# A planned order for four chained attention layers, searched anew: same operations, other orders, engines and banks

## The chip, the cores and the metric

The kernel runs on one core of a Trainium2 chip. The core has five instruction streams that run side by side and meet only through semaphores: TensorE (PE; matrix products into eight PSUM banks), ScalarE (ACT), VectorE (DVE), GpSimd (POOL) and SyncE (SP, which issues most transfers). The metric is device time in microseconds (us) of one execution; lower is better. Times are given as the median of several runs on the same chip.

## What is computed

Four layers with a residual around each, on x of 2048 tokens by 512 features, 32 heads of 16 features:

```python
x = x + A(layernorm(x), A_wqkv, A_wo)
x = x + B(layernorm(x), B_wqkv, B_wo)
x = x + A(layernorm(x), A_wqkv, A_wo)
x = x + B(layernorm(x), B_wqkv, B_wo)
# A, linear attention: phi(t) = where(t > 0, t + 1, exp(t)) + 1e-6
#   kv = sum over tokens of phi(k) v;  z = sum of phi(k);  o = phi(q) kv / (phi(q) z + 1e-6);  o @ wo
# B, sliding window of 256 keys, causal: o = softmax(q k / 4 inside the window) v;  o @ wo
```

## The kernel before, in words

**Tiles.** The 2048 tokens are 16 tiles of 128. A norm (`norm`, L363) is statistics on VectorE (L367, L368), an addition of epsilon on GpSimd or VectorE (L369), a power -1/2 on GpSimd (L370), the scaling on VectorE (L371) and a transposition, which is a DMA transpose that SyncE issues (L377) or, for ten of them, four PE products (L383) with an eviction (L390). Products of a token tile with weights are written by `tok` (L406: two instructions of 512 columns for each half of the contraction) or `feat` (L420: eight of 128 columns for each half). In A layers, keys and queries go through `phi` (exponential on ScalarE L429, then VectorE L430 and L431). In B layers, scores are products in 32-row tiles of PE (L638; the far part of the window L677 or L680), exponentials on ScalarE (L648, L690), masks on VectorE (L656, L700, L709) or GpSimd (L708), values `pv` (L729, up to 24 instructions of 34 columns), a reciprocal and a scaling (L740, L741), the product with wo (L406) and the residual (L574). Keys and values pass through two rearranging transfers each (`kd` L600, `vd` L619). The second B layer streams its finished tiles to the output (L847, L782).

**What sets the order.** Plan builds a graph of 2542 operations, the same in every version: names, what each reads and writes, which engines may do it. `place` (the function printed at the end of this section) then takes from a packed string, TABLE, three things: the global order of the operations, the engine of each, and the PSUM bank of each tile. Each engine runs its own operations in that order; `synchronise` puts a semaphore wait wherever an operation needs another engine's result or the bank that an earlier tile held. SyncE's queue is in order too: a transfer whose wait is not met holds back all behind it. One more wait comes from `place`: a GpSimd operation that is not in the list SHORT waits for the last VectorE operation of the kinds E1, xn, mk, mf that stands ahead of it in the global order.

```python
    order = [ops[raw[2 * k] + 256 * raw[2 * k + 1]] for k in range(n)]
    for o in ops:
        o.eng = ("PE", "ACT", "DVE", "POOL", "SP")[raw[2 * n + o.i]]
    for k, x in enumerate(tiles):
        x.banks = [raw[3 * n + k]]
    for o in order:
        if o.eng == "POOL" and o.name not in SHORT and wide and wide not in o.deps:
            o.deps.append(wide)
        if o.eng == "DVE" and o.name in WIDE:
            wide = o
```

**Names used below.** An operation is called by its name and its number in the order of building: fill0 to fill9 are ten products with no use for the result (L268), which keep PE busy at the start, behind nine more of the same kind (L984); k24 is the first half of the first layer's key product of tile 12 (two instructions, L406), k26 and k27 those of tile 13; T12 is the DMA transpose of tile 12 (L377) and xn12 its scaling (L371); g is the product of normed x and phi(k) (L481); wp0 to wp7 copy and permute B's weights (L355) and zero0 to zero4 clear buffers (L803, L818, L820); s38 and s111 are groups of scores (L638); k40, k41 are key products of the second A layer, bv18, bv19 value products of the first B layer (all L406); spread3 is the product that spreads reciprocals to heads (L556), pqd12 to pqd15 the four VectorE multiplications that read it (L563), bve9 the eviction of bv18 and bv19 (L395); bk52 is a half of a key product of the second B layer (L420, eight instructions); outp0 to outp14 are the output transfers of its first 15 tiles (L847).

Of the kernel before, what the change touches and what calls it, by code (L numbers as in the profile page):

```python
# [223 lines left out]
class Plan:  # L224
# [639 lines left out]
    r"-N}%?_Ew~MLpedY&Gw>S1syz@+B~;(TS-1;7z#BLZ;Z=H72~d$@RTG*)26YbZ!F?D3BViO&1yK*+Eo4-gR3epF{Rlrn1Qk(5QUz5ZRaj+KSyU3G)k84K",
    r"s>rH{DypKWf=~#mKvb1fy@O;bxpFGH8VzHhw#urqsbVU-%Aty@5~`$%rgEyvkW!^kxl}1tTIE({RaI3@l~Gkx0jQ($KwhY;>Zt~*vZ}6XsFtdgYOQLjT",
    r"B^QU18ZR&6ow*D6xyhUs;z3I8mo4yiE6K!tBTN6HB&9rde{Ip-~#M}{cr#}sDm(CjZq=s5j=*uYM!bFW7Rk{QjJm<VVxSU)~iEM5+<mLYQDMzlhgur85",
    r"XJ|s-xPVp1@O>tlq;1n4)H=nQE3=q&BL>YKfYvrm5+wlez+%)Mm9`9aRU^QuPcvt1fDeI;OU$t?Hm!sk*9<uu9c})vBB7u0FvswOj?m;J8A~R=3n~6#|",
    r"2);OdSl1t-)=bxQS6Au$wQRoB#QbzN;!C9ouZhSMs9I;;+<N9wUEh1*p~6-t%H&=>}HsGaJGx~ZaL42+4-)C<*9mBF&OOYK(A)jf4zmBTZtmkNt})LB&",
    r";o~m=|fm)+3sEg{nTB~AX0!)Mn@uez{XYirAq-tU<ysK`gI2aG(Vr@K&=WrCB#|wB7M`IEkgYj{nN`|RaYV}UNS0B_H^-;Z5KdPTpQcR8^AsnVr;V}Y^",
    r"#c?<uBVt;W0uy5etcaDcGVWE8FeRo_bulug!i*RN>){oZ2`{S&I1w9Q6|9Q&F*9bt)OZPF;bp9Y)$o&QhAnV5&cV6Z96zf`_(gqHKP$jS*ch{7Hq4GW@",  # L870
    r"Gf4#?^Hv)hxf4wHpN#;AtK>xH5q?UQ*bJ_!mHQ@b7E_}hS#y2`d;-`jOA5Zte`5YN-7Q3z+9LXJ7X8@iVH9uw#0>)8@pk5%z$|?FXlr*jZrZ_7QjUq4H",
    r"u(9i%YNv&PRvKuqRH#7-}h|$CxUX>V*YyIZnqJ7+b|rE3go*!mYRsx8n|6iG5UGRUOyhIxLL+)Bx2RS7U!w1jEr<T#rSu7>1_^R2(BxB#KP)@EJbG7kC",
    r"4A;x62cd+-N*gEz4<RiU?d3m@SVe29;+5B9~ExEG^PRLY~OQa_AFc~yTLfcaE@)ebx0U7CdhaS%Sm0_q;M$4)pHhv1JGpAt|)x=#buAoU%-#u?NRXJR#",
    r"~PBo||?Zf@}3OC?Jyn_dDCVj%sIEyyn_qYXXQ40EkUvW0gp`Q^bB`HEmMX4zX#iH1hjN;Hx9ENGAHXX#Il$?g+2poy&XfAEW=oEuuQhjPb4=@8A!ozq3",
    r"(^5{#MYpjbJ)lhVkXlkkBFas9s1+rmN0gqJgftz+%(Rl)QXLwsT2mWpPl@RmKBgzMidIuQ>Oeo?dwhrSs4mr`yp)gf(+4a-9jOU5rB2kD3X-9&)Sa5qa",
    r"Xf(^@g#Pm=G2eYQGc38mK+76`LuxI(kVQR184&Ur$RK4TF`nbOkHRb^`IgYf{Icx8bpI>Ej^_nw3&v|7Ro|dX)6_{5>%2F(jr<+*=PxEqwTbmcF;1~NF",
    r"gZ{4N)W1P?eoRQy3~mKhPT*uHMoxwTpIB4%$PBI58*Tq@0Y`P-!YdWhpF`qsCO8l5+~~NiV4vrQ~NcjC#{|G@M4zNE$_r=oRgw*R-Gd&~y5p4$~2OL8I",
    r"v?9is#EiN4Sp9z$bkFYTnYypEgmJNiuTX&il}7Tl5#Q7S%8<LLyQq!08n0r&M@8mH(qt>?^~g@2-~oSJ{6kJO4=a~md3!)aNVIRuB~P@IF?a!wA-nhz3",
    r"kE<QtN=^UM>c07S5QXUS&VR;fwrYV$;^Ko7d$KkmM=jIEvfs1i|UQX$`D6gOl{3HLw@3=h|;6i+nE>UsL#+RuqZ{$rJfy;4cF3%OXAQ$G%+?Ts>f9}9t",
    r"xg!tcPW+xfa7C`fmH7%);eI@T2lF5v!iF7ZXUh>e5@+OK9GRnVRlZ8s=sNY_o*b2X@fIG*qj)Ms<7w1~qw{E<PJ4MD-=O^*gM0HwF2SF;6lda?e3Pnib",  # L880
    r"*{lRxg_u4ojjC>@h%R|lejcb=2~2v4{>*%!ee+Uf9B!5mACN--p;q^HXY_V+>MX$F+Ra{`3u+Mqdbj|b1aU{cPI`|=aYPnm0aK%tR*hbWRzK4hU0ld-~",
    r"gZJQ+$SvSUJtt`37I);1WXWa{~@34f!UY<=cFV@9<qd$WB5_SZT!fcs7TTIoz1%@;v^^;pIL@lwk5RXOrwQmO&!Od|to{c^v1EP_l@da8n-7&G-R7<VX",
    r"CNpKxS}BCVvgw2`B7iKEIfxy*YwJ}2Ob99?$vaY@LFc>*utrTj!#u5b*ACXwW+h=h|ka*gB4Q+~$FcsZ}&n37+f^9z0^&!wPT<=7HW;!6TaD7oZ?6p%!",
    r"cSdvI?$tx!$kDQcKa!$@mEGaBSWF@cS3sOifN^vPFB_*F+lFL#-DoST5A*=bNd?%HpvUHVV(q6hqDXAh=rJLlGYEoU=Nm5BB9i)czmX6X%l1p2uK(FMr",
    r"RHXirLQ+a9NiBV(uk@4er4n_Q9x^}%${_iH-*6g9D{r}{%$51lOXkS}dCA}LD}K%2b7?6ngJp=6k(x47W=Sn6FGFRRq?7bATjoePSt`q9xtx|Wa#m_f9",
    r"a$)grLNSI`qDt&$$R-A86>l;kd?AZ7ReGBE+b^5jFQo^R@TW6vR<;t8`&UN<f^QejFMHZiPCFiqr8<dGFCpyCut~+q_K>X@zO*#$#vN*TjYk^lv{FJ>g",
    r"xu2t8DXLX{5Ky4%sQqrG?y)rqWFA$^_XZtfz_SA7#4yB)eszOp-lvNHWP}nIU^+pG=W^GFA4=0ck1s<*+=EgYr<0$Rl|y_4H@?B3boU$)~gETsptbqx0",
    r"$l`ezBQL+Bhjx6Y|S7u4BwcCEG1g>*yRNEg<fbr)Sk57kyX-B>r#O?5L}R7cdqbXOflht-jEbKOF>)ZO$PJy#FcA$2R=PPf+`bVnUZch{|TC*4Mm(9?B",
    r"j9a;C#J#{bLTesDH^hg~{kJ91v3>`(!)1&nmT};o^vvhIYSC7>Lba*{bm(b(%AU#A6)=_mo-Csx0CG~h+T9?uj^h8}oZ_-<ISv_B0(O30m9mXus3-wmL",
    r"O@}qx^(1{w&(@3db-h@JGdJ{2eM>LV`}AZzMNiX3Oi@$J?AHhM4!ujS)wlId9p0?d>-8NSO&2#MOmrPXf2U*W*E*JdrDN+jI<Agjmg;3XqS>wY>VtZ@j",  # L890
    r";G`6je4qns-Njd=DFUWBbzAZrCy;|>OJ~<{YL+wALxgAmA<P#>d*R-KCBbyg!+j7q!a0qrj&W1SL=KFkiM_K=(r}Hd8>ca$Mp#v-yGGa^%;FqpVB|+$2",
# [179 lines left out]
```

## Time and profile before

| what | value |
|---|---|
| median of 3 runs | 410.21 us (409.73 to 410.4) |
| span of the profiled execution | 408.2 us |
| PE, DVE, ACT, POOL busy in it | 396.0, 347.9, 344.4, 113.8 us |
| PE work (instructions) | 7997 products and as many weight loads |
| transfers | 67654 packets, 37.88 MB |
| instruction packets on queue q8 | 63, of 1.03 MB in all |

The profiled execution has only its span as a time: from the first to the last instruction of the program. The median of the runs is 2.0 us above it; that is what lies around the span. A row of the timeline gives the start, the length, the engine and line, what is written and read, how many instructions were merged, and in brackets the idle time of the engine before it with what ended that. Products on PE overlap: a row of PE begins some 0.17 us before the one ahead of it has ended, so a pause shows as a late start even where the bracket is small.

### The profile page before, as it was taken

How to read it: one execution, taken by the hardware profiler on the slowest of the kernel's cores; microseconds unless marked ns; L12 is line 12 of the kernel's file. 1: busy time of each engine (PE TensorE's matmuls, PEld its weight loads, DVE VectorE, ACT ScalarE, POOL GpSimd, SP SyncE). 2: the span in 40 equal slices, each digit the busy share in tenths (PEclk: the TensorE clock that was granted, in tenths of full speed). 3: DMA queues.
4: the chain of work that ended last, by engine and by line, in shares of the span. 5: the costliest groups of instructions: out<-in, count | busy, mean ns of one | idle time of the engine just before them, and what ended most of it. 6: DMA issues, size and time to landing. Idle time of an engine off the chain costs nothing.

```text
span 408.2 us, 18082 instructions
## 1 busy us (share of the span) xinstructions
PE 396.0 (97%) x7997; PEld 263.4 (65%) x7997; DVE 347.9 (85%) x808; ACT 344.4 (84%) x443; POOL 113.8 (28%) x194
## 2 busy tenths in 40 slices
PE   8999999999999999999999999999999999999996
PEld 3654676666575566666666777676757766576664
DVE  5998799999998999888977789988898778876685
ACT  3655579999999999999998355999998999999992
POOL 3553632112253343330503202122123201302212
PEclk9999999999999999999999999999999999999999
DMA  8754014923242934344231100364225542442543
GB/s 247 243 118 104 2 42 121 184 56 97 65 119 52 132 73 108 75 104 106 62 69 36 29 2 28 89 127 78 71 76 130 143 83 61 66 121 62 118 109 104
DMA packets 67654, 37.88 MB, mean 93 GB/s; under 512 B 48248, under 2 KB 62712, under 8 KB 67576
## 3 DMA queue, kind: packets, MB, share of 16 engines
q1 hardware_dynamic: 67184, 35.67, 38.1%
q8 instruction: 63, 1.03, 1.1%
q0 software_dynamic: 384, 1.05, 0.8%
q14 instruction: 15, 0.12, 0.1%
q10 hardware_dynamic: 8, 0.00, 0.0%
HBM read 6.29 MB, written 2.10 MB: 21 GB/s over the span
## 4 chain that ended last, share of the span: by engine, by line
PE 81%; ACT 10%; DVE 7%; DMA 1%; issue 1%; DVEq 0%
PE ps L406 27%; PE ps L420 20%; PE ps L729 15%; PE ps L638 8%; ACT pb L648 7%; PE ps L680 2%; PE ps L481 2%; ACT pb L690 1%; DVE XQ L563 1%; PE ps L677 1%; DMA XQ<-vp 1%; PE ps L984 1%; PE ps L457 1%; PE ps L543 1%; PE ps L268 1%
## 5 line engine op out<-in xcount | busy, mean ns | idle before, releaser
L648 ACT ACTIVATE pb<-ps 128x1024 bf16<-128x1024 f32 (+3 forms) x224 | 198.2, 966 | 7.4 <-PE ps L638 6.2
L729 PEld LDWEIGHTS ps<-vB,pb 128*128 128x128 bf16 x2560 | 77.6, 96 | 11.5 <-issue 4.2
L729 PE MATMUL ps<-vB,pb 128*128 128x34 bf16 x2560 | 83.2, 177 | 0.3
L420 PE MATMUL ps<-xT,wBp 128*128 128x128 bf16 x1024 | 68.6, 219 | 0.1
L420 PEld LDWEIGHTS ps<-xT,wBp 128*128 128x128 bf16 x1024 | 58.4, 98 | 9.6 <-issue 4.0
L708 POOL TENSOR_SCALAR_AFFINE_SELECT pb<-pb 128x1024 bf16<-128x1024 bf16 x34 | 39.1, 1149 | 84.0 <-DVE pb L700 31.9
L429 ACT ACTIVATE tE<-ps 128x512 bf16<-128x512 f32 x64 | 38.1, 606 | 18.4 <-PE ps L406 12.1
L638 PE MATMUL ps<-XQ,kB 32*128 32x256 bf16 (+2 forms) x1024 | 48.7, 262 | 3.3 <-ACT pb L648 0.6
L574 DVE TENSOR_TENSOR xres<-ps,xres 128x512 bf16<-128x512 f32 x63 | 43.1, 685 | 9.6 <-PE ps L406 9.1
L690 ACT ACTIVATE pb<-ps 128x1024 bf16<-128x1024 f32 x50 | 49.0, 1048 | 1.3 <-PE ps L680 1.0
L406 PE MATMUL ps<-wA,XQ 128*128 128x512 bf16 x192 | 49.2, 380 | 0.7 <-DMA XQ<-vp 0.6
L369 POOL TENSOR_SCALAR ve<-mv 128x1 f32<-128x1 f32 x49 | 11.8, 240 | 127.9 <-DVE mv L368 126.9
L370 POOL TENSOR_TENSOR rs<-ve,negh 128x1 f32<-128x1 f32 x64 | 37.9, 592 | 32.0 <-DVE ve L369 27.5
L367 DVE BATCH_NORM_STATS2 stats<-xres 128x6 f32<-128x512 bf16 x64 | 43.8, 685 | 2.8 <-DMA xres<-in_A_x_dram 2.1
L638 PEld LDWEIGHTS ps<-XQ,kB 32*128 32x128 bf16 x1024 | 15.7, 92 | 31.4 <-ACT pb L648 8.3
L420 PE MATMUL ps<-XQ,wA 128*128 128x128 bf16 x512 | 34.4, 219 | 0.0
L406 PE MATMUL ps<-wBv,xT 128*128 128x512 bf16 x128 | 34.3, 380 | 0.0
L406 PE MATMUL ps<-M,XQ 128*128 128x512 bf16 x128 | 33.3, 380 | 0.2
L420 PEld LDWEIGHTS ps<-XQ,wA 128*128 128x128 bf16 x512 | 30.1, 98 | 5.1 <-issue 0.6
L406 PE MATMUL ps<-wBo,oT 128*128 128x512 bf16 x124 | 32.7, 380 | 0.6 <-DVE vp L431 0.4
L656 DVE TENSOR_TENSOR pb<-pb,tri 128x512 bf16<-128x512 bf16 x68 | 27.7, 419 | 3.7 <-ACT pb L648 3.1
L741 DVE TENSOR_TENSOR o<-ps,rc 128x256 bf16<-128x256 f32 x64 | 27.0, 422 | 1.7
(114 smaller groups left out, 545.9 us busy)
## 6 DMA issues: line engine op xcount, KB each, us to landing
vB<-vS SPq DMA_DIRECT2D x64, 136.0 KB, 2.6
kB<-vp SPq DMA_DIRECT2D x64, 128.0 KB, 2.2
wA<-in_A_wqkv_dram SPq DMA_DIRECT2D x3, 512.0 KB, 5.2
xres<-in_A_x_dram SPq DMA_DIRECT2D x2, 512.0 KB, 4.8
pb<-in_B_wqkv_dram SPq DMA_DIRECT2D x1, 1024.0 KB, 6.9
out_dram<-xres POOLq DMA_DIRECT2D x8, 128.0 KB, 2.5
out_dram<-xres SPq DMA_DIRECT2D x7, 128.0 KB, 2.0
xres<-in_A_x_dram SPq DMA_DIRECT2D x3, 256.0 KB, 5.3
```

Of the source, the lines that this page charges most:

```text
L367: self.on("DVE", "stats", lambda e: e.bn_stats(K.stats[:, t, :], K.xres[:, t, :]), key, dve(512), rd=[("xres", t)], wr=[("stats", t)])
L370: self.pow = self.on("POOL", "pow", lambda e: e.tensor_tensor(K.rs[:, t, :], K.ve[:, t, :], K.negh[:], ALU.pow), key + 0.03, (640, 690), r ...
L406: m = e.matmul(K.ps(ps), lhs(c), rhs(c), start=c == 0, stop=c == 3)
L420: m = e.matmul(K.ps(ps)[:, f * P:(f + 1) * P], w(c, f), xT(c), start=c == 0, stop=c == 3)
L429: self.on("ACT", "E", lambda e: e.activation(K.tE[:, s, :], K.ps(ps), ACT.Exp, bias=0.0), key, act(512), wr=[("tE", s)], ps=[ps])
L574: self.on("DVE", "res", lambda e: e.tensor_tensor(K.xres[:, t, :], K.ps(po), K.xres[:, t, :], ALU.add), key, dve(512), rd=[("xres", t)], w ...
L638: m = e.matmul(K.ps(ps[gq])[:, ns * i:ns * i + ns], K.kB[rows, j % 4, 2 * f + b, :, :], K.XQ[rows, f, q:q + ns], start=True, stop=True, ti ...
L648: return e.activation(out(h, ns).rearrange("p (f g) c -> p f g c", f=n), i, ACT.Exp, bias=0.0, scale=0.25)
L656: return e.tensor_tensor(x, x, K.tri[:, 0, :].unsqueeze(1).to_broadcast([P, 4 * n, 64]), ALU.mult)
L690: return e.activation(o.rearrange("p (f g) b c -> p f g b c", g=2), i, ACT.Exp, bias=0.0, scale=0.25)
L708: return e.affine_select(out=x, in_=x, compare_op=ALU.is_ge, fill=0.0, base=-2, pattern=[[0, 16], [-2, 64]], channel_multiplier=1)
L729: m = e.matmul(K.ps(ps)[:, 34 * u:34 * u + 34], K.P((b // 2) % rp)[:, f, gq % 2 * 2 + gq // 2, o:o + P], K.vB[:, (b // 2) % 4, b % 2, r, : ...
```

## The change

Only TABLE is another string (two lines shorter, so the lines behind it move up by two: L984 is L982). The graph, the emitted instructions' shapes and the waits' rules are the same.

```diff
 TABLE = (
-    r"c-qZa1K1|VvaT*P*0yciwr$(CZQHhO+qTW@CcDXcb7%hV<eVfoo0F4!@AKUGhSk+o?^{*fGyMUCh3765goc+c9E6835CI|rLPAiG2oggihztY|-3#}`C",
...
+    r"c-qx@1GFW{(r!jXMn-1awr$(CZQHhO+qP}nwrykjuj(`X{+YScbMMT%YrXaARPL<(W#9``?y7a3I;BvBQlS;7V2adTci)9jPaG?)j1m=Bg;DpMQxDuj7hHu^",
...
 )
```

Unpacked, and set beside the old one by names:

- **Engines.** 52 operations change engine. By counts (before to after): wp on ACT 6 to 2, on POOL 2 to 6; zero on ACT 3 to 1, on POOL 2 to 4; recb on ACT 5 to 3, on DVE 3 to 5; outp on POOL 8 to 9, on SP 7 to 6; mf on DVE 17 to 16, on POOL 39 to 40; eps on POOL 49 to 48, on DVE 15 to 16; bqe on DVE 22 to 21. In all ACT has 442 to 437 operations, DVE 807 and 807, POOL 190 to 196, SP 235 to 234.
- **PE order.** 868 operations; 88% stand in the same sequence, with the same 333 changes between tile shapes. The ten fills were spread over the first 15 us (two ahead of the first transposition, three between the first two, five behind); now seven stand ahead of the first transposition, two between the first and the second, one behind.
- Sequences on PE at places that are spoken of below (before, then after):

```text
B  g16 q8 q9 g18 k26 g20 k24 k25 k27 g19
A  g16 g18 k26 k27 q8 q9 g20 k24 k25 g19

B  s37 bk21 k40 k41 spread3 bv18 bv19 s38 aout24
A  s37 bk21 bv18 bv19 spread3 k40 k41 s38 aout24

B  pv89 s118 bv50 bv51 s111 bk52 bk53 bq54
A  pv89 s118 bk52 bv50 bv51 s111 bk53 bq54
```

- **VectorE around the second place:** bke10 mk28 pqd15 pqd12 becomes bke10 pqd12 pqd15. s38 waited for both pqd12 and pqd15; now it waits for pqd12, and for bve9 on ScalarE, which stands ahead of E36 instead of behind it.
- **From 345 us on** PE's sequence differs in one place (pv103 ahead of pv100) and ScalarE's in two swaps of neighbours and the operation of the last point below; VectorE's sequence changes in most stretches (286 of its 807 operations lie elsewhere).
- **SyncE, first layer:** the load of A_wo stood behind T7, the third DMA transpose, and now stands behind T12, the ninth; the transposes keep their sequence (T13 ahead of T12).
- **The end.** Before: SP issued outp14 (the last whole tile) and the two halves of tile 15; POOL ended with outp12, outp7, outp13. After: SP issues the two halves alone; POOL ends with outp12, outp13, outp14, outp7. The first eviction of the last transposition (oTe1, L395) moves from ACT to DVE, behind the residual of tile 13 (L574), which moves behind the scaling of the half tile before.

More of the change, by code (lines that the diff above doesn't have):

```diff
@@ L864 @@
[L864 to L879, printed above, removed]
```

90 lines of the change are left out of this document (52 added, 38 removed).

## The prediction

> **What bounds the kernel now.** I read the page first, for the engines' shares, then who waited for whom on PE, then the sums by stretch, and then the timeline at the places that the change touches.
>
> ```profile
> span 408.2 us, 18082 instructions
> PE 396.0 (97%) x7997; PEld 263.4 (65%) x7997; DVE 347.9 (85%) x808; ACT 344.4 (84%) x443; POOL 113.8 (28%) x194
> ```
> ```profile
> 0.00:10.00 10.00, 8.75 (x38) 3.81 (x39) 5.86 (x16) 3.00 (x4) 3.41 (x14) 1.00 0.80 244
> ...
> 400.00:410.00 10.00, 4.72 (x111) 3.34 (x109) 3.93 (x9) 1.46 (x4) 2.38 (x5) 0.99 0.35 107
> ```
>
> The first fence is the page, the second the sums by stretches of 10 us (length; busy time of PE, weight loads, DVE, ACT, POOL; granted clock; share and GB/s of the transfers). PE is busy 396.0 of 408.2 us, so no new order can take away more than the 12.2 us of its idle time. Of these, 10.0 - 8.75 = 1.25 lie at the start and 8.2 - 4.72 = 3.5 at the end, behind the last products, where the order hardly changes. That leaves 12.2 - 1.25 - 3.5 = 7.45 us: the floor is about 410.21 - 7.45 = 402.8.
>
> ```profile
> 115.00:140.00 25.00, 24.10 (x539) 16.16 (x535) 22.14 (x55) 24.90 (x29) 7.45 (x14) 1.00 0.49 90
> 341.50:386.00 44.50, 41.93 (x1175) 29.62 (x1171) 32.69 (x75) 44.02 (x52) 8.99 (x11) 1.00 0.45 97
> ```
>
> These two rows (same columns, other stretches) say that part of the 7.45 is out of reach. From 115 to 140 us ScalarE is busy 24.90 of 25.00, and from 341.5 to 386 us 44.02 of 44.50, while PE idles 0.90 and 2.57: there PE waits because ScalarE is full. The change leaves ScalarE's operations and nearly their sequence there as they are, so what PE gains inside such a stretch it waits for at its next exponential. About 7.45 - 0.90 - 2.57 = 4.0 us are open to a better order.
>
> ```profile
> PE ps L406 <- DMA XQ<-vp: 0.6, 1, 0.6
> ...
> PE ps L638 <- DVE XQ L563: 0.4, 1, 0.4
> ```
>
> Who waited for whom on PE (total, times, longest): no wait above 0.6 us but the start's, and one that names a transfer. So the change is judged wait by wait.
>
> **The change part by part.**
>
> *Transfers and instruction packets.* The landing times do show what the new search is about:
>
> ```profile
> q1 hardware_dynamic: 1697, 0.41, 45.0%
> ...
> XQ<-vp SPq DMA_TRANSPOSE x4, 2.4
> ```
> ```profile
> q8 instruction: 1, 0.02, 2.8%
> ...
> XQ<-vp SPq DMA_TRANSPOSE x2, 3.3
> ```
> ```profile
> DMA to landing us min/median/max: 2.4/2.6/5.3
> ```
>
> The first is the transfers' view from 25 to 29.5 us: four transposes, no packet of queue q8 (q1, their own, is the only queue listed), 2.4 us to landing. The second is from 30.5 to 33.5 us: one q8 packet, and the median of two transposes is 3.3. The third is the source view of all 84 transposes. A transfer that meets a packet is late by about 0.9 us, at most 2.9. PE pays for it at one place:
>
> ```profile
> 29.82 0.41 DVE L371 TENSOR_SCALAR vp<-xres,mv,rs 128x512 bf16<-128x512 bf16 x1
> ```
> ```profile
> 33.66 0.59 PE L481 MATMUL ps<-vp 128*128 128x512 bf16 x2
> 34.84 1.47 PE L406 MATMUL ps<-wA,XQ 128*128 128x512 bf16 x6 [0.59 <-DMA XQ<-vp]
> ```
>
> xn12 ends at 30.23 on VectorE and T12 follows it. Two products take 0.43 (the pair below, 9.28 to 9.71), so k24 could have started at 33.66 + 0.43 = 34.09; it started at 34.84, and 0.75 us went. In the new order k27, one more pair, stands ahead of k24: 0.43 more cover. The A_wo load behind T12 instead of ahead of T8 frees SyncE earlier, but VectorE is the one that T12 waits for: between its gate (the second tile pair's load) and xn12 the new order puts the same work on it. If T12 meets its packet again, 0.75 - 0.43 = 0.32 stay; if not, nothing stays. Bounds of this part: -0.75 to 0; I take **-0.43**.
>
> *The fills.* With two fills ahead, the first transposition started at 5.92. Now seven stand there:
>
> ```profile
> 5.07 1.06 PE L268 MATMUL ps<-kB 128*128 128x512 bf16 x2
> 5.92 0.63 PE L383 MATMUL ps<-ident,vp 128*128 128x128 bf16 x4
> 6.34 1.15 PE L268 MATMUL ps<-kB 128*128 128x512 bf16 x3
> 7.33 0.39 PE L383 MATMUL ps<-ident,vp 128*128 128x128 bf16 x4
> 7.55 1.89 PE L406 MATMUL ps<-wA,XQ 128*128 128x512 bf16 x8
> 9.28 0.59 PE L268 MATMUL ps<-kB 128*128 128x512 bf16 x2
> 9.71 1.06 PE L420 MATMUL ps<-XQ,wA 128*128 128x128 bf16 x16
> 10.61 0.39 PE L383 MATMUL ps<-ident,vp 128*128 128x128 bf16 x4
> ```
>
> The first two take 5.92 - 5.07 = 0.85, the next three 7.33 - 6.34 = 0.99, later ones 0.215. Seven take 0.85 + 0.99 + 0.43 = 2.27, so T0 comes at 7.34, T1 at 7.34 + 0.22 + 0.43 = 7.99, and k0 at 7.99 + 0.22 + 0.215 = 8.42. Before, k0 came at 7.55 with five fills still to pay, 5 x 0.215 = 1.08, which is 8.63 on the same count. PE has no pause up to 34 us in either case, so the moved fills cost and save **0**; bounds -0.2 (8.42 against 8.63) to +0.3 (an exponential later in front of VectorE, which is full there). The Trainium skill, TensorE: Matmul & The Clock Gate, section on the clock gate, says that the warm-up is a budget of about 3.4 us of time and not a number of products; by it fills moved to the front warm nothing sooner. The trace agrees: the pitch goes from 0.43 to 0.215 between 6.3 and 7.3 us, whatever is run. The sum stays 0 by both.
>
> *The scores s38.*
>
> ```profile
> 138.73 1.04 PE L406 MATMUL ps<-wA,XQ 128*128 128x512 bf16 x4
> 139.74 0.40 PE L556 MATMUL ps<-rec,spread 32*128 32x128 bf16 x16
> 140.07 1.04 PE L406 MATMUL ps<-wBv,xT 128*128 128x512 bf16 x4
> 141.54 0.40 PE L638 MATMUL ps<-XQ,kB 32*128 32x256 bf16 x8 [0.42 <-DVE XQ L563]
> ```
> ```profile
> 140.19 1.29 DVE L563 TENSOR_TENSOR XQ<-ps,XQ 128x512 bf16<-128x512 f32 x2 [0.30 <-PE ps L556]
> ```
> ```profile
> 138.48 2.03 ACT L648 ACTIVATE pb<-ps 128x1024 bf16<-128x1024 f32 x2
> 140.28 0.72 ACT L429 ACTIVATE tE<-ps 128x512 bf16<-128x512 f32 x1
> 141.15 0.66 ACT L395 ACTIVATE vS<-ps 128x512 bf16<-128x512 f32 x1
> 141.99 1.02 ACT L648 ACTIVATE pb<-ps 128x1024 bf16<-128x1024 f32 x1 [0.18 <-PE ps L638]
> ```
>
> Before, s38 waits for pqd15 and pqd12, the two operations of 1.29 us behind spread3, and starts at 141.54. After, bv18 and bv19 come ahead of spread3 and pqd12 is the first. bv18 and bv19 are as long as k40 and k41, so spread3 starts where it did, 139.74; pqd12 takes pqd15's place and ends at 140.19 + 0.69 = 140.88 (half of 1.29, and the overlap); PE is there at 139.74 + 0.33 + 0.86 = 140.93 (the pieces of the rows above). A new wait enters: bve9 must be done, and it stands behind the two exponentials (end 140.51) on ScalarE, where the next row starts at about 140.4: 140.4 + 0.66 = 141.06. So s38 starts near 141.1 instead of 141.54. Queued behind bve9 is E36, 0.72, which ends by 141.7 and whose reader is VectorE's next step of phi; the exponential of s38 then starts near 141.6, not 141.99. Both engines gain: **-0.4**; bounds -0.45 and 0.
>
> *The scores s111.*
>
> ```profile
> 326.02 0.37 PE L638 MATMUL ps<-XQ,kB 32*128 32x224 bf16 x8
> 326.32 1.04 PE L406 MATMUL ps<-wBv,xT 128*128 128x512 bf16 x4
> 327.50 0.37 PE L638 MATMUL ps<-XQ,kB 32*128 32x224 bf16 x8
> ```
>
> Four products with the change to a 32-row shape take 139.74 - 138.73 = 1.01, so s111 could start at 326.32 + 1.01 = 327.33 but starts at 327.50: it waits for the exponential of s118. bk52, eight products of 128 columns or half of the 10.61 - 9.71 that sixteen take, 0.45 us, now lies between. **-0.17**; bounds -0.17 and 0.
>
> *What moves off ScalarE and SyncE.* Four wp, two zero and two recb leave ScalarE. The wp and zero lie where ScalarE is not the bound (18.22 of 30 us busy):
>
> ```profile
> 35.00:65.00 30.00, 29.91 (x397) 19.56 (x396) 26.77 (x55) 18.22 (x30) 12.35 (x25) 1.00 0.22 55
> ```
>
> GpSimd is busy 12.35 of the 30 us, so the moved copies, 0.75 each by the row below, lie beside PE's work; if the constants that they push back came late for the first spread, at most 4 x 0.75 = 3.0 would show at PE. I count **0**.
>
> ```profile
> L355 POOL COPY wBp<-pb 128x512 bf16<-128x512 bf16 x2 | 1.5, 754 | 2.4 <-DVE tE L430 2.3
> ```
>
> *The end.* The first eviction of the last transposition goes to VectorE behind the residual of tile 13 and the last scaling, some 0.5 us later than on ScalarE, and the products that read it stand behind one more transposition. GpSimd issues outp14 and outp7 last. I count **+0.1**; bounds 0 and +0.5 (by the rows below an output that GpSimd issues lands in 2.5 us, one of SyncE's in 2.0).
>
> ```profile
> out_dram<-xres POOLq DMA_DIRECT2D x8, 128.0 KB, 2.5
> out_dram<-xres SPq DMA_DIRECT2D x7, 128.0 KB, 2.0
> ```
>
> The Trainium skill, DMA: Bandwidth & Descriptors, section on issuing engines, says that transfers issued by SyncE, ScalarE and GpSimd run on the same sixteen engines, so another issuer saves issue time alone. By it moving outputs to GpSimd shortens no landing; the two medians above agree, and the sum stays.
>
> *The other moves* (286 on VectorE, 88 of 235 on SyncE) cannot be priced one by one. All open waits of PE give the lower bound, -4.0 with the terms above. The upper bound is new waits of the size of k24's, 0.75 each. I take 0, the nearest to the rows: PE idles 0.09 of 30 us from 35 to 65, so most moves are covered.
>
> **Sum:** -0.43 - 0.4 - 0.17 + 0.1 = -0.90. The span goes from 408.2 to 407.3, and with the 2.0 us around it (410.21 - 408.2) the median to about **409.3**.
>
> **The rivals.**
>
> *More than that (0.13).* The search may have found, in VectorE's many moves, the other waits too. All of the 4.0 us would give 406.2, my terms give 409.3; I put this case halfway, at 407.7. For it: VectorE's new order packs masks into its idle time ahead of waits. Against it: the largest waits left stand at full stretches of ScalarE.
>
> *It washes out (0.21).* The change doesn't do what it says: packets come at fixed counts of PE's instructions, 88% of PE's order is the same, so T12 meets the same packet, and a wait saved at s38 comes back at the next exponential. Then 410.2, within 0.5. For it: ScalarE has only 0.10 us of idle time just ahead of s38. Against it: ScalarE itself waits 0.18 for s38.
>
> *Slower: transfers with less cover (0.20).* SyncE's queue is in order, and a transfer that meets a packet holds its reader by 0.9 us or more, up to 2.9. The new order moves 88 transfers. Where a moved one both has less cover and meets a packet that the search put elsewhere, PE waits as at k24, 0.75 each. One such wait nearly cancels my sum, two pass the old time; at three it is 409.3 + 3 x 0.75, about 411.5. For it: the packets' places follow PE's real progress, which the search only estimated. Against it: the old order, made without this, had one such wait in 408 us.
>
> **How the numbers follow.** My own sum has 0.46. 0.2% of 410.21 is 0.82, about what a measurement of this kernel can tell from no change; 409.3 lies just beyond it, and of my sum's 0.46 I put 0.34 below 409.39 and 0.12 above. Faster by over 0.2%: 0.13 + 0.34 = 0.47. Within 0.2%: 0.21 + 0.12 = 0.33. Slower: 0.20. The range goes from 407.0, below the rival of more, to 411.5, the slower rival with three waits; beyond them I leave less than 0.2.
>
> **What would show it right or wrong.** In the changed kernel's profile: the wait of PE's L406 for the transfer XQ<-vp is gone or below 0.35; the wait of 0.42 before the scores behind spread3 is gone, and ScalarE's idle time there too; the scores of s111 follow PE's products without a wait; PE's idle sum falls from 12.2 to about 11; ScalarE is as full from 341 to 386 us. The prediction is wrong if PE shows several new waits for transfers (kB, vB, XQ, oT or xT), if VectorE idles between 10 and 33 us, or if the last output lands later behind the last residual than before.

## The result, and the profile after

The changed kernel takes **413.28 us** (median of 20 runs, 411.35 to 414.49) against 410.19 (20 runs) of the kernel before: ratio 1.0073, 95% interval 1.0056 to 1.0089. It is slower by 3.1 us; forecast were 409.3, with 411.5 as the upper end. The page of the changed kernel, span and busy time:

```profile
span 411.7 us, 18011 instructions
...
PE 387.8 (94%) x7924; PEld 262.5 (64%) x7997; DVE 349.1 (85%) x808; ACT 341.0 (83%) x438; POOL 120.2 (29%) x200
```

7997 weight loads stand beside 7924 products: 73 records of products are missing in this trace (all of products of 512 columns), so PE's 387.8 is too small and its idle time cannot be read from it. VectorE, with as many operations as before, is busy 1.2 us longer (349.1 against 347.9). Who waited for whom on PE, after:

```profile
PE ps L680 <- DVE o L741: 0.9, 1, 0.9
...
PE ps L420 <- DMA xT<-xn: 0.8, 1, 0.8
PE ps L638 <- DMA kB<-vp: 0.7, 1, 0.7
...
PE ps L729 <- DVE pb L656: 0.5, 1, 0.5
...
PE ps L406 <- DMA XQ<-vp: 0.3, 1, 0.3
```

The wait for T12 (0.6) and that of the scores for `DVE XQ L563` (0.4) are gone. Among the new ones are three waits for transfers (kB, xT and XQ) and one for a mask (pb), and the wait of the scores s142 for `DVE o L741` has grown; before, it was

```profile
PE ps L680 <- DVE o L741: 0.6, 1, 0.6
```

To see where the 3.1 us went I took, from both traces, the start of the same product wherever both kernels have run the same set of PE operations up to there, and subtracted: the **lag**. A step in it is time lost or won since the row above. The same table for three of the experiments below (us):

| from the row above to (start before) | changed | GpSimd apart (a_apart2) | transfers (a_cover) | both (a_mend) |
|---|---|---|---|---|
| k21 (29.74) | +0.32 | +0.52 | +0.11 | -0.42 |
| g19 (36.15): k24 and T12 | -0.59 | -0.59 | -0.59 | -0.58 |
| k30 (39.57) | +1.04 | +0.49 | +1.56 | +0.70 |
| bq4 (65.68): T18 | +0.20 | +0.56 | 0.00 | 0.00 |
| s6 (71.58): kd2 | +0.78 | +0.30 | +0.01 | +0.01 |
| pv12 (97.81): xn22, mk13 | +1.14 | +0.17 | +1.14 | +0.17 |
| k36 (117.95): T24 | +0.67 | +0.85 | +0.18 | +0.21 |
| s33 (129.99) | 0.00 | 0.00 | +0.03 | +0.01 |
| s38 (141.54) | -0.33 | -0.33 | -0.33 | -0.32 |
| bk40 (269.23): T52 | +0.79 | -0.05 | -0.05 | -0.04 |
| bq54 (328.71) | -0.01 | -0.02 | +0.01 | +0.71 |
| s142 (374.24): mk111 | +0.39 | +0.06 | +0.40 | +0.09 |
| pv114 (386.36) | -0.85 | +0.03 | +0.34 | +0.04 |
| bout64 (404.38) | -0.32 | -0.33 | -0.33 | -0.32 |
| lag there | +3.21 | +1.67 | +2.46 | +0.26 |

Each column is one execution, and executions differ at the start. The kernels below that equal the changed one up to k21 (a_sp, a_apart, a_apart2) reach it at 29.20, 29.36 and 30.26 us, those that equal the kernel before (b_gains, b_gains2, b_gains3) at 29.20, 30.40 and 29.27. So the first row, which is part of every lag below it, is not shown to come from the change; the other rows are steps and don't contain it.

**Two kinds of loss.** The first is VectorE beside GpSimd. VectorE's timeline of the changed kernel (97 to 101 us), then GpSimd's and PE's there:

```profile
97.19 0.29 DVE L430 TENSOR_SCALAR tE<-tE 128x512 bf16<-128x512 bf16 x1
97.69 1.39 DVE L371 TENSOR_SCALAR xn<-xres,mv,rs 128x512 bf16<-128x512 bf16 x1 [0.21 <-POOL rs L370]
99.01 0.67 DVE L431 SCALAR_TENSOR_TENSOR vp<-ps,tE 128x512 bf16<-128x512 f32 x1
```
```profile
97.79 1.15 POOL L708 TENSOR_SCALAR_AFFINE_SELECT pb<-pb 128x1024 bf16<-128x1024 bf16 x1
```
```profile
99.83 0.40 PE L638 MATMUL ps<-XQ,kB 32*128 32x256 bf16 x8 [0.48 <-DVE vp L431]
100.69 0.97 PE L729 MATMUL ps<-vB,pb 128*128 128x34 bf16 x32 [0.47 <-DVE pb L656]
```

xn22, which lasts 0.40 elsewhere, lasts 1.39: until just after the mask mf2 on GpSimd ends at 98.94. All that follows on VectorE is 0.99 late, and PE waits for it twice, at s17 and pv12. Such stretches come nine times in this trace (xn15, E124, E126, xn22, xn31, mk63, mk111, mk109, mk120: 4.8 us over the median of their kinds) and twice before (0.8 us). The groups of instructions show it as a mean that has moved, in the kinds that read and write bf16 in SBUF alone. Before, then after:

```profile
L656 DVE TENSOR_TENSOR pb<-pb,tri 128x512 bf16<-128x512 bf16 x68 | 27.7, 419 | 3.7 <-ACT pb L648 3.1
...
L431 DVE SCALAR_TENSOR_TENSOR XQ<-ps,tE 128x512 bf16<-128x512 f32 x32 | 21.6, 681 | 0.4
...
L371 DVE TENSOR_SCALAR xn<-xres,mv,rs 128x512 bf16<-128x512 bf16 x48 | 19.4, 404 | 1.1 <-POOL rs L370 0.7 <-DMA XQ<-xn 0.2
```
```profile
L656 DVE TENSOR_TENSOR pb<-pb,tri 128x512 bf16<-128x512 bf16 x68 | 28.3, 428 | 4.5 <-ACT pb L648 4.4
...
L431 DVE SCALAR_TENSOR_TENSOR XQ<-ps,tE 128x512 bf16<-128x512 f32 x32 | 21.8, 682 | 0.4
...
L371 DVE TENSOR_SCALAR xn<-xres,mv,rs 128x512 bf16<-128x512 bf16 x48 | 20.9, 436 | 2.3 <-POOL rs L370 2.3
```

L371 goes from 404 to 436 ns and L656 from 419 to 428; L431, which reads f32 from PSUM, stays (681, 682). The Trainium skill, SBUF — State Buffer, section "Who interferes with whom", says that the only port shared between engines is one pair that VectorE and GpSimd hold in turn for a whole instruction, and names which VectorE operations need it; the trace agrees with the kinds that stretch and those that don't. The rule in `place` guards one side: a GpSimd operation waits for the last such VectorE operation ahead of it in the order, and nothing holds the next VectorE operation behind it.

The second kind is late transfers. SyncE's timeline of the changed kernel around T52, the transfers' view of 266 to 273.5 us, and PE:

```profile
266.91 3.47 SPq L619 DMA_DIRECT2D vB<-vS  x3
270.42 1.29 SPq L377 DMA_TRANSPOSE xT<-xn  x1
```
```profile
q8 instruction: 1, 0.02, 1.4%
...
vB<-vS SPq DMA_DIRECT2D x3, 136.0 KB, 4.1
...
xT<-xn SPq DMA_TRANSPOSE x3, 2.7
```
```profile
273.24 0.33 PE L420 MATMUL ps<-xT,wBp 128*128 128x128 bf16 x3 [0.77 <-DMA xT<-xn]
```

The transposition T52 (270.42) could have gone out at 269.1, when xn52 was done. Ahead of it in SyncE's queue stand three copies, issued at 266.91, 267.72 and 268.31; the instruction packet lies from 268.27 to 269.99, and the queue issues nothing more until 270.42. In this trace 20 of the 212 issues of transposes and copies last over 1.5 us, all of them beside a packet; of the 159 beside none the longest lasts 1.31. So a packet delays not only the landing (4.1 us for the copies) but also the next issue. Before, xn52 was done 5.7 us ahead of bk40 (263.5, 269.23), now 4.1 (269.1, 273.24), 0.8 of it PE's wait: the same kind of delay met less cover. T24 is alike (issued at 116.89, landed 4.5 us later beside the packet of 118.2, k36 waits). s6 is another case: the load of B_wo stands directly ahead of kd2, and kd2 lands 4.3 us after its issue instead of 2.0:

```profile
68.14 0.58 SPq L291 DMA_DIRECT2D wBo<-in_B_wo_dram  x1
68.77 0.51 SPq L600 DMA_DIRECT2D kB<-vp  x1
```
```profile
73.32 0.40 PE L638 MATMUL ps<-XQ,kB 32*128 32x256 bf16 x8 [0.72 <-DMA kB<-vp]
```

Of 212 transposes and copies that SyncE issues for tiles, 80 overlapped a packet before and 78 after (a packet lies in the time from 1.2 us after the issue to the landing, in the two traces): the new order has not moved the transfers out of the packets' way.

**The clock adds to the first kind.** mk111 is stretched from 0.42 to 1.25 us (at 376.60), and the wait of s142 behind it grows from 0.60 to 0.94 us. In the trace above the granted clock stays at 1.00 behind this wait. In the trace of a_sp below, where the same place waits 0.93, it is 0.50 from 377.04 to 380.45; on its page that is slice 37 of 40:

```profile
PEclk9999999999999999999999999999999999998999
```

3.41 us at half the clock make a mean of 0.996 over the span. Of the changed kernel's 20 executions ten have a mean granted clock of 0.992 or 0.996, with a median of 414.15 us, and ten of 0.998 to 1.000, with a median of 412.58. Of a_apart2's twelve, where s142 waits 0.60 again, none is below 0.998, and of 123 executions of the kernel before nine are. So an estimate of 0.7 us of the 3.1 (413.28 - 412.58) is the clock and not the waits themselves; the profiled execution, at 1.000, does not contain it. That the wait of s142 is where the clock fell in each of the ten is likely and not shown, and why the same wait is followed by half the clock in one execution and not in another stays open.

### The profile page after: what moved, and what is told of

It is laid out like the page before. It is cut to its first block, busy times and chain, and to the rows that moved or that the text cites. A ratio compares the mean times of both kernels' runs of the same rounds, so it can differ in the third digit from the quotient of the medians.

```text
span 411.7 us, 18011 instructions
## 1 busy us (share of the span) xinstructions
PE 387.8 (94%) x7924; PEld 262.5 (64%) x7997; DVE 349.1 (85%) x808; ACT 341.0 (83%) x438; POOL 120.2 (29%) x200
## 4 chain that ended last, share of the span: by engine, by line
PE 62%; DVE 18%; ACT 11%; DMA 4%; issue 2%; POOL 1%; SPq 1%; POOLq 0%
PE ps L406 20%; PE ps L420 15%; PE ps L729 13%; ACT pb L648 7%; PE ps L638 7%; DVE stats L367 3%; DVE vp L431 2%; PE ps L680 2%; DVE xres L574 2%; ACT pb L690 2%; DVE XQ L431 2%; DMA xres<-in_A_x_dram 2%; DVE tE L430 1%; DVE xn L371 1%; DMA kB<-vp 1%
## 5 line engine op out<-in xcount | busy, mean ns | idle before, releaser
L708 POOL TENSOR_SCALAR_AFFINE_SELECT pb<-pb 128x1024 bf16<-128x1024 bf16 x37 | 43.9, 1187 | 83.3 <-DVE pb L700 41.0
L406 PE MATMUL ps<-wA,XQ 128*128 128x512 bf16 x178 | 45.7, 379 | 3.1 <-DVE mv L368 0.5
L574 DVE TENSOR_TENSOR xres<-ps,xres 128x512 bf16<-128x512 f32 x63 | 43.0, 684 | 6.2 <-PE ps L406 5.4
L370 POOL TENSOR_TENSOR rs<-ve,negh 128x1 f32<-128x1 f32 x64 | 36.9, 577 | 33.6 <-DVE ve L369 28.9
L406 PE MATMUL ps<-wBv,xT 128*128 128x512 bf16 x109 | 30.6, 380 | 2.0 <-issue 1.3
L656 DVE TENSOR_TENSOR pb<-pb,tri 128x512 bf16<-128x512 bf16 x68 | 28.3, 428 | 4.5 <-ACT pb L648 4.4
L406 PE MATMUL ps<-M,XQ 128*128 128x512 bf16 x112 | 30.0, 380 | 1.8 <-issue 0.8
L406 PE MATMUL ps<-wBo,oT 128*128 128x512 bf16 x104 | 28.4, 380 | 3.4 <-DVE rc L740 1.4
L406 PEld LDWEIGHTS ps<-wA,XQ 128*128 128x128 bf16 x192 | 16.3, 97 | 20.8 <-issue 2.2
```

Source lines behind the costliest of these rows:

```text
L370: self.pow = self.on("POOL", "pow", lambda e: e.tensor_tensor(K.rs[:, t, :], K.ve[:, t, :], K.negh[:], ALU.pow), key + 0.03, (640, 690), r ...
L406: m = e.matmul(K.ps(ps), lhs(c), rhs(c), start=c == 0, stop=c == 3)
L574: self.on("DVE", "res", lambda e: e.tensor_tensor(K.xres[:, t, :], K.ps(po), K.xres[:, t, :], ALU.add), key, dve(512), rd=[("xres", t)], w ...
L656: return e.tensor_tensor(x, x, K.tri[:, 0, :].unsqueeze(1).to_broadcast([P, 4 * n, 64]), ALU.mult)
L708: return e.affine_select(out=x, in_=x, compare_op=ALU.is_ge, fill=0.0, base=-2, pattern=[[0, 16], [-2, 64]], channel_multiplier=1)
```

## Experiments

Each kernel is one of the two with a few operations moved in the decoded order. The device, at the end of the file; an entry reads (operation, after or before, operation):

```diff
-    order = [ops[raw[2 * k] + 256 * raw[2 * k + 1]] for k in range(n)]
+    order = arranged(ops, [ops[raw[2 * k] + 256 * raw[2 * k + 1]] for k in range(n)])
+def arranged(ops, order):    # named[...]: operations by name and number
+    for a, where, b in MOVES:
+        order.remove(named[a])
+        order.insert(order.index(named[b]) + (where == "after"), named[a])
```

**GpSimd apart from VectorE (a_apart, a_apart2).** Theory one against theory two.

```diff
 a_apart: the changed kernel
+('c211', 'before', 'c221'), ('c101', 'after', 'wp5'), ('mf2', 'after', 'xn22'), ('mf7', 'after', 'xn31'),
+('mf6', 'after', 'mf7'), ('mf26', 'after', 'mk60'), ('mf46', 'after', 'mk105'), ('mf49', 'after', 'mf50')
 a_apart2: the same, but
-('mf26', 'after', 'mk60')
+('mf26', 'after', 'div29') and mf26 on VectorE
```

> The changed kernel with eight GpSimd operations at other places of the order (c101, c211, mf2, mf6, mf7, mf26, mf46, mf49), each now behind the VectorE operation that it ran beside; nothing else moves. In the changed kernel's trace seven VectorE operations (xn15, E124, E126, xn22, xn31, mk63, mk111) that overlap a GpSimd mask or fill by more than 0.2 us last 0.2 to 1.0 us longer than their kind, 4.3 us in all. Theory one, the loss is VectorE slowed beside GpSimd: the PE waits of k28 and k30 (0.51 and 0.52 us), s17 and pv12 (0.55 and 0.53) and most of s142's 0.56 go, so 1.3 to 2.4 us off the changed kernel's 413.3, to 411 to 412. Theory two, the loss is late transfers: within 0.5 us of 413.3, because the stretched operations only use time that PE would wait elsewhere.

> The changed kernel with the GpSimd operations apart from the VectorE operations, as in the first set, and mf26 on VectorE behind div29 so that it no longer holds pv62; transfers and the rest as in the changed kernel. Theory one, VectorE slowed beside GpSimd: the first set gained 0.7 us with a fault of 1.06 us in it, so 1.6 to 1.9 us off 413.3, 411.4 to 411.7. If those 1.06 only covered another wait, it stays at 412.5.

a_apart: 412.57 us (ratio to the kernel before 1.0057, 1.0027 to 1.0086), a_apart2: **411.45** (1.0024, 0.9998 to 1.0050). In a_apart mf26 held pv62 for 1.06 us, a new wait that this edit brought; with mf26 on VectorE instead the moves give 1.8 of the 3.1 us, as theory one had it. This includes the clock's part. VectorE's stretched time falls from 4.8 to 0.5 us. The same place in a_apart2, VectorE and GpSimd:

```profile
97.24 0.41 DVE L371 TENSOR_SCALAR xn<-xres,mv,rs 128x512 bf16<-128x512 bf16 x1 [0.21 <-POOL rs L370]
```
```profile
97.73 1.15 POOL L708 TENSOR_SCALAR_AFFINE_SELECT pb<-pb 128x1024 bf16<-128x1024 bf16 x1 [0.52 <-DVE xn L371]
```

The mask now waits for xn22, which lasts 0.41. In the table the rows of xn22 and mk111 lose nearly all their loss, that of k30 half. But s6 and bk40 also lose 0.48 and 0.84, though no transfer was moved, bq4 loses 0.36 more, and the gain at pv114 is gone. The two kinds of loss are not independent, and the split below is one of sets of moves, not of causes at each row.

**Transfers (a_sp, a_cover).**

```diff
 a_sp: the changed kernel
+('wBo0', 'after', 'vd2'), ('T24', 'before', 'kd14'), ('xn52', 'before', 'stats53'), ('T52', 'before', 'vd35')
 a_cover: the same, and
+('xn14', 'before', 'stats15'), ('eps18', 'before', 'pqd6'), ('pow18', 'before', 'pqd6'),
+('xn18', 'before', 'pqd4'), ('T18', 'before', 'vd0'), ('q7', 'before', 'g1')
```

> The changed kernel with the load of B_wo behind vd2 instead of ahead of kd2, T24 ahead of kd14, T52 ahead of vd35 and xn52 two VectorE operations earlier, ahead of stats53; GpSimd as in the changed kernel. Theory two, late transfers: the waits of s6 (0.79 us, for kd2 that landed 4.3 us after its issue, right behind that load), of k36 (0.49, for T24) and of bk40 (0.84, for T52) go, 2.1 us off 413.3, to about 411.2. Theory one, VectorE beside GpSimd: at most 0.5 us off, since the waits return at the stretched VectorE operations.

> The changed kernel with the transfers' set alone: the B_wo load behind vd2, T24 ahead of kd14, T52 and xn52 earlier, xn14 and xn18 with T18 earlier, and q7 ahead of g1; GpSimd as in the changed kernel. Theory two, late transfers: the first, smaller set gained 0.5; with bq4's 0.2 to 0.9 and g1's 0.4 gone too, 1.0 to 1.6 off, 411.7 to 412.3. The two sets together came to 410.47, 2.8 below 413.3; if the two causes add, this and the GpSimd set make about 2.8 between them.

a_sp: 412.78 (1.0060, 1.0035 to 1.0086), a_cover: **412.26** (1.0053, 1.0031 to 1.0075). a_sp gave 0.5, far less than the 2.1 that theory two expected: its three waits went, and bq4's wait for T18 grew from 0.2 to 0.8. With that mended too, a_cover gives 1.0; its interval overlaps the changed kernel's (1.0056 to 1.0089), so by itself this gain is at the edge of what these runs can tell. The table shows why not more: 2.5 us are won (k21, bq4, s6, k36, bk40), but k30 loses 0.5 more, and the gain of 0.85 that the changed kernel had at pv114 turns into a loss of 0.34. Most of that row (0.62 of the 0.85) is a pause on PE that nothing in the trace releases, inside a group of scores; here in a_cover:

```profile
PE ps L638 <- issue: 0.8, 1, 0.8
```

It was 0.4 at the same group (s145) before and absent in the changed kernel. It comes between two instruction packets in a run of short products; whether PE waits for its instructions there is not shown.

**Both (a_both, a_mend, a_best).**

```diff
 a_both: the changed kernel with a_apart's and a_sp's moves
 a_mend: with a_apart2's and a_cover's moves
 a_best: a_mend, and
+('g6', 'before', 'k10'), ('E124', 'after', 'xn15'), ('phi24', 'after', 'E124'),
+('c100', 'after', 'wp3'), ('oT18', 'before', 'kd45')
```

> Both sets of moves in the changed kernel. If the two losses are separate and together are the cause, they add: 3.5 to 4.4 us off 413.3, 409 to 410, at or below the kernel before. If one of them hides the other, the time is that of the better of the two alone. If the loss lies in neither, it stays above 412.5.

> The changed kernel with both sets of moves, and with what the last traces still showed beside them: mf26 on VectorE behind div29 (on GpSimd behind mk60 it held pv62 for 1.06 us, a fault of the first two sets), xn14 ahead of stats15, pow18, xn18 and T18 earlier (PE waited 0.5 to 0.9 us for T14 and T18, each landing late beside an instruction packet), and q7 ahead of g1 (0.41). If these waits are the loss, 1.06 + 0.5 + 0.7 + 0.4 come off the 411.76 of both sets together: about 409.1, below the kernel before. If waits that go return at other transfers and at full stretches of ScalarE, it stays above 410.3.

> The changed kernel with all sets of moves, and with four places that its last trace still showed: g6 ahead of k10 (0.43 us waited for phi8), E124 and phi24 directly behind xn15 and c100, c101 later (k28 and k30 waited 0.39 and 0.31 behind a stretched xn15), and oT18 ahead of kd45 (0.65 at bout36). If these waits go without new ones, 1.0 to 1.8 off 410.47, 408.7 to 409.5, faster than both kernels. If packets and full stretches give them back, 410 to 411.

a_both: 411.76 (1.0042, 1.0025 to 1.0058), with mf26's 1.06 in it. a_mend: **410.47** (1.0004, 0.9984 to 1.0024). So the two sets of moves add as far as the noise lets one tell: 1.8 and 1.0 alone, 2.8 together, of 3.1. The intervals of a_apart2 and a_mend lie below the changed kernel's. a_best: 410.51 (1.0001, 0.9987 to 1.0015), no gain more, as the expectation's second case had it. In its trace bout36's wait is gone, but k28 waits 0.30 for a transfer, E130 (0.96 us) is now stretched beside a GpSimd operation, and the pause without a releaser is 0.71 instead of 0.54. Nothing beats the kernel before. a_mend's page:

```profile
span 408.8 us, 18079 instructions
...
PE 395.8 (97%) x7997; PEld 262.3 (64%) x7997; DVE 346.1 (85%) x809; ACT 340.8 (83%) x438; POOL 119.7 (29%) x199
```

Here all records are there; PE is busy 395.8 of 408.8, as it was before, and VectorE 3.0 us less than in the changed kernel.

**The prediction's three swaps alone (b_gains, b_gains2, b_gains3).**

```diff
 b_gains: the kernel before
+('k27', 'after', 'k26'), ('bv18', 'before', 'spread3'), ('bv19', 'before', 'spread3'), ('k40', 'after', 'spread3'),
+('k41', 'after', 'k40'), ('pqd12', 'before', 'pqd15'), ('bve9', 'before', 'E36'), ('bk52', 'before', 'bv50')
 b_gains2: and PSUM banks 5 for spread3's part of pqd15, 3 for bv18 and bv19
 b_gains3: and banks 3 and 5 for spread3's parts of pqd12 and pqd15, 0 for bv18 and bv19, as in the changed kernel
```

> The kernel before with only the three swaps that the prediction priced: k27 directly behind k26 (ahead of k24), bv18 and bv19 ahead of spread3 with k40 and k41 behind it, pqd12 ahead of pqd15 and bve9 ahead of E36, and bk52 ahead of bv50. The prediction's sum for them: -0.43 - 0.4 - 0.17 = -1.0 us, to about 409.2. Washed out at the next full stretch of ScalarE: 409.8 to 410.4. Slower would say that a swap costs more at its place than it saves.

> The kernel before with the three swaps again, and with the two PSUM banks that the second swap needs: the bank of spread3's part for pqd15 and that of bv18 and bv19 are exchanged, so that s38 waits for pqd12 and bve9 and no longer for pqd15 (without that, s38's wait stayed 0.49 us). The prediction's sum: -1.0. From the first try, k24 gives -0.25 and s111 -0.24, and g25, k30, s34 and bq54 took 0.9 back: then 409.8 to 410.2, and s38 alone moves by -0.3 to -0.4.

> The kernel before with the prediction's three swaps, and with spread3's parts for pqd12 and pqd15 and the tile of bv18 and bv19 in the banks that they have in the changed kernel (3, 5 and 0). The last try put bv18 into a bank that was held for another 0.99 us; these banks are free by then. Now s38 has no wait above 0.15 us. The prediction's sum -1.0 would give 409.2; with what the first try showed to come back at g25, k30, s34 and bq54 (0.9 of it), 409.8 to 410.1.

410.16 (1.0004, 0.9984 to 1.0024), 412.17 (1.0055, 1.0030 to 1.0080) and 411.17 (1.0018, 0.9991 to 1.0045). In b_gains s38 still waits 0.49: it needs the bank that pqd15 reads, which the swap alone does not change. b_gains2 frees it at the price of 0.99 at bv18, whose new bank is held. b_gains3 has the banks right, PE's timeline:

```profile
139.68 0.40 PE L556 MATMUL ps<-rec,spread 32*128 32x128 bf16 x16
140.01 1.04 PE L406 MATMUL ps<-wA,XQ 128*128 128x512 bf16 x4
140.98 0.40 PE L638 MATMUL ps<-XQ,kB 32*128 32x256 bf16 x8
141.48 1.04 PE L406 MATMUL ps<-M,XQ 128*128 128x512 bf16 x4
142.66 1.04 PE L406 MATMUL ps<-wA,XQ 128*128 128x512 bf16 x4
143.86 0.32 PE L677 MATMUL ps<-XQ,kB 32*128 32x64 bf16 x20 [0.16 <-DVE xres L574]
```

s38 starts at 140.98 instead of 141.54, 0.56 earlier, of which 0.30 was there at s37 already. But the next three groups, which started at 141.87, 142.74 and 143.70, stand at 141.48, 142.66 and 143.86: the gain is used up within 3 us, and more. The same happens at k24 (-0.25, then +0.30 at g25 and k30) and s111 (-0.22, then +0.29 at bq54).

**The packets' places (b_shift, b_q1, b_q3, b_full; a_shift, a_q1, a_q3, a_full).** The warm-up is lengthened by 64, 32, 96 or 128 products, each with a weight load: half, a quarter, three quarters of a packet, a whole one. 7997 products and loads each over 63 packets make 254 instructions a packet.

```diff
-                    for _ in range(9):
-                        e.matmul(self.PS[:, SPARE, :], warm[:, 0:P], warm, start=True, stop=True)
+                    for _ in range(73):
+                        e.matmul(self.PS[:, SPARE, 0:64], warm[:, 0:P], warm[:, 0:64], start=True, stop=True)
 q1: 41 of 112 columns; q3: 105 of 44; full: 137 of 34; in q3 and full the fills have 34 columns instead of 512
```

> The same 73 warm-up products in the kernel before. If its order has cover for late transfers wherever a packet falls, the time stays within 0.5 us of 410.2. If its 410.2 rests on where its packets happen to fall, new waits for transfers appear on PE and it goes to 411 to 413.

> The changed kernel with 73 warm-up products of 64 columns in place of 9 of 512 (9 x 512 = 4608 columns against 73 x 64 = 4672, no result is used). PE runs 128 more instructions (64 loads and 64 products) ahead of the first transposition, half of the 254 that lie between two instruction packets, so all packets meet the work half a packet earlier; nothing else moves. If the place of the packets decides which transfer is late, the waits of k10 (T5), bq4 (T18), k36 (T24) and bk40 (T52), 2.0 us in all, go, others come, and the time moves by 0.8 us or more either way. If the loss doesn't hang on the packets, the time stays within 0.6 us of 413.3.

> The kernel before with 137 warm-up products of 34 columns in place of 9 of 512, that is 128 more, 256 more PE instructions: one whole packet instead of half of one. The ten fills are cut from 512 to 34 columns to make room; no result of either is used. If the 7 us that half a packet cost come from where the packets fall, a whole packet puts them back to their places and the time is 409.5 to 411.5. If they come from the longer warm-up or from more instructions as such, it stays at 415 or more.

> The changed kernel with 41 warm-up products of 112 columns: 64 more PE instructions, a quarter of a packet. If the changed order was made for other packet places than the real ones, some other place should suit it: below 412.5 at one of the quarter and three quarters. If its transfers have less cover wherever the packets fall, it is slower than the kernel before with the same shift, at both.

> The changed kernel with 105 warm-up products of 44 columns, and the fills of 34 columns: 192 more PE instructions, three quarters of a packet. As for the quarter: below 412.5 if this place suits the changed order, 415 to 420 if, as at half a packet, more transfers are late.

> The kernel before with the same quarter of a packet. It took 410.2 at its own place, 417.1 at half a packet more and 411.1 at a whole one. If its order only suits one place, 412 to 415 here; if half a packet is a special case, 410 to 411.

> The kernel before with the same three quarters of a packet: 412 to 415 if its order only suits one place, 410 to 411 if half a packet is a special case.

> The changed kernel with 137 warm-up products of 34 columns and fills of 34 columns, a whole packet more, as was done to the kernel before (411.06 there). If the packets' places alone make the difference between the shifts, the changed kernel comes back from 418 to 420 to 413 to 414.5.

| packets later by | order before, us (ratio) | changed order, us (ratio) | changed less before |
|---|---|---|---|
| 0 | 410.19 | 413.28 (1.0056 to 1.0089) | 3.1 |
| 1/4 | 411.72 (0.9995 to 1.0056) | 414.10 (1.0055 to 1.0099) | 2.4 |
| 1/2 | 417.10 (1.0139 to 1.0201) | 419.44 (1.0178 to 1.0249) | 2.3 |
| 3/4 | 414.12 (1.0041 to 1.0115) | 418.12 (1.0130 to 1.0211) | 4.0 |
| 1 | 411.06 (1.0004 to 1.0045) | 414.14 (1.0057 to 1.0123) | 3.1 |

Ratios are to the kernel before, as 95% intervals. The packets' places are worth 6.9 us to the one order and 6.2 to the other, and a whole packet puts both back to within 0.9. Part of this is the clock: all six executions of b_shift have a mean granted clock of 0.992 to 0.996. Both orders do best at their own place and worst at half a packet; the changed order is 2.3 to 4.0 above at each of the five. So it is not slower for having been made for other packet places: none of those tried suits it. What half a packet does to the kernel before, its waits on PE, then its timeline on PE and the sums of two stretches:

```profile
PE ps L406 <- DMA XQ<-xn: 1.1, 1, 1.1
PE ps L420 <- DVE mv L368: 1.0, 1, 1.0
PE ps L406 <- DMA oT<-o: 1.0, 1, 1.0
PE ps L680 <- issue: 0.8, 1, 0.8
```
```profile
100.07 0.40 PE L638 MATMUL ps<-XQ,kB 32*128 32x256 bf16 x8 [0.29 <-DVE o L741]
101.61 1.86 PE L406 MATMUL ps<-wA,XQ 128*128 128x512 bf16 x4 [1.14 <-DMA XQ<-xn]
103.27 1.48 PE L406 MATMUL ps<-M,XQ 128*128 128x512 bf16 x3
```
```profile
99.00:101.60 2.60, 0.97 (x31) 0.50 (x28) 2.56 (x6) 1.94 (x3) 0.00 (x0) 0.95 0.29 80
101.60:104.00 2.40, 2.39 (x6) 0.85 (x7) 1.38 (x4) 1.35 (x2) 0.00 (x0) 0.50 0.51 105
```

Two transfers that had cover now hold PE for 1 us each, and one wait is paid twice: behind the 1.14 us the granted clock is 0.50, and four products that take 1.04 elsewhere take 1.86.

## Why the prediction was wrong

- **k24 and T12: right in size, in part by luck.** Forecast -0.43 (0 to -0.75), measured -0.59. The forecast put it on one more pair of products as cover; what happened is its other branch. T12 met no packet: the packet of 32.45 in the kernel before came at 35.64, T12 landed 2.4 us after its issue instead of 4.2 (33.38 instead of 34.80), and k24 follows without a wait, as it would have without the pair:

```profile
33.69 1.06 PE L420 MATMUL ps<-XQ,wA 128*128 128x128 bf16 x16
34.58 0.59 PE L481 MATMUL ps<-vp 128*128 128x512 bf16 x2
35.01 1.03 PE L406 MATMUL ps<-wA,XQ 128*128 128x512 bf16 x4
```

- **Fills: 0, and no run contradicts it.** Seven fills took 6.97 - 5.07 = 1.90 us, not 2.27, so k0 came at 8.06 instead of the forecast 8.42; the same order gave 7.57 to 8.74 in other traces. The +0.32 by k21 lies within what executions differ there. Of the waits in it, that of k10 for T5 (0.48) is absent in a_sp and longer in a_cover, so it is not the order's alone; that of g1 (0.41) is gone with q7 ahead of it.

```profile
5.07 2.07 PE L268 MATMUL ps<-kB 128*128 128x512 bf16 x7
6.97 0.39 PE L383 MATMUL ps<-ident,vp 128*128 128x128 bf16 x4
...
8.06 1.89 PE L406 MATMUL ps<-wA,XQ 128*128 128x512 bf16 x8
```

- **s38: right, -0.33 for -0.4**, by the steps named (pqd12, then bve9), and with the banks of the new order, which the forecast didn't name and without which the wait stays (b_gains). That it lasts is owed to the rest of the new order: in the kernel before the same swap is used up within 3 us.
- **s111: right in size (-0.21 for -0.17) and worth nothing**: bq54 gives 0.20 back. That is the rival "it washes out", at this one place.
- **The end: +0.3 for +0.1.** From the end of the last residual to the end of the span are 411.7 - 408.89 = 2.8 us, before 408.2 - 405.69 = 2.5.

```profile
408.01 0.88 DVE L781 TENSOR_TENSOR xres<-ps,xres 128x256 bf16<-128x256 f32 x2 [0.57 <-PE ps L775]
```
```profile
404.80 0.89 DVE L781 TENSOR_TENSOR xres<-ps,xres 128x256 bf16<-128x256 f32 x2 [0.51 <-PE ps L775]
```

The sum of these terms was -0.90; measured they come to -0.59 - 0.33 - 0.01 + 0.3 = -0.63. Two gains that I had not seen, -0.85 at pv114 and -0.32 at the end of the table, would have made it more. What failed are two other steps.

- **"What moves off ScalarE and SyncE", counted 0, failed.** Its cover was GpSimd's free time (12.35 of 30 us). GpSimd had the time; the price was VectorE's. In the new order, with four wp and two zero more on GpSimd, c101 and c211 run beside E124 and E126, which took 0.94 and 0.50 us instead of 0.28 (before, E126 alone was stretched, to 0.92). That the moved copies pushed c101 and c211 there is likely and not shown. I asked who waits for GpSimd and not who runs beside it.
- **"The other moves", taken as 0, failed**, and this is the step that decides. "PE idles 0.09 of 30 us, so most moves are covered" was read from the kernel before; cover is a property of an order and goes with it. Measured: undoing the GpSimd moves gives 1.8 us back (a_apart2), some 0.7 of it by the clock, undoing the transfers 1.0 (a_cover), both 2.8 (a_mend).
- **The rival "slower: transfers with less cover"** had the second mechanism and its price: 0.78, 0.67 and 0.79 in the rows of s6, k36 and bk40 against 0.75 forecast, and it reckoned with three of them. I gave it 0.20. The first mechanism, the larger one, stood in no rival, and neither did the clock, so even its 411.5 lay below the result.
- **The packets matter more than I allowed**: their places are worth 6 to 7 us. The new order did not use that: as many transfers overlap packets as before. One reading of the landing times was wrong: the 5.3 us that I took for the latest transfer beside a packet is T21 (issued at 71.42), which also stood 0.63 us behind the load of B_wo (70.79).

## What to carry to other kernels

Where an order is searched anew, price what it does to covers that the old order had, not only the waits that it removes: count, on each side of the change, who runs beside whom (a GpSimd mask beside a bf16 operation of VectorE cost up to 1 us of VectorE here) and how long each transfer is done ahead of its reader. In this kernel, whose tensor engine is 97% busy, swaps that gained 0.2 to 0.3 us each were given back within a few microseconds. Look at the granted clock of every execution, not only of the profiled one: a wait of 0.9 us that is followed by half the clock in some of them moves the median. And this kernel's time hangs on where its instruction packets fall: test a change, and any added instruction, by a shift of the packets before trusting a difference of a few us.

## What the runs showed of the hardware

- **VectorE operations that read bf16 from SBUF and GpSimd masks or fills hold each other up.** The nine that began inside a mask or fill, or up to 0.10 us ahead of it, ended only after it: 0.2 to 1.0 us more (xn22 0.40 to 1.39). Those that began 0.15 us or more ahead kept their length (mf9, mf42, mf55: 0.68 to 0.69), and the mask beside them lasted 1.47 to 1.53 us instead of 1.15 (mf8, mf47, mf54). Operations that read f32 from PSUM beside the same masks keep their length (ten of L431 in the changed trace: 0.68 to 0.69).
- **An instruction packet holds SyncE's next issue too** (T52: 1.3 us after xn52; only beside packets did an issue last over 1.5 us), not only the landings.
- **128 tensor instructions more at the start cost 6.2 to 6.9 us, 256 cost 0.9** (the table of the packets' places).
- **A wait of PE can be paid twice.** Behind 1.14 us of waiting the granted clock was 0.50 over the 2.4 us shown (b_shift) and products took nearly twice their time; behind 0.97 us in the same trace it stayed 1.00, and behind 0.93 us at s142 it was 0.50 in one trace (a_sp) and 1.00 in another (a_cover). The Trainium skill, TensorE: Matmul & The Clock Gate, section on the clock gate, names an idle window of about 3.4 us; PE was idle far less here: in 99 to 101.6 us of b_shift it was busy 0.97 of 2.60, and in the 3.41 us ahead of a_sp's half clock 2.48. So by these traces a window need not be idle throughout.
